# Cached attention on one core: new instruction lists, odd score steps as 64-row matmuls, query weights of 128 columns

## The chip, the core and the metric

The kernel runs on one core of a Trainium2 chip. The core has five engines with instruction streams of their own: TensorE (PE; its weight loads are listed as PEld), VectorE (DVE), ScalarE (ACT), GpSimd (POOL) and SyncE (SP), which here issues all loads and stores. TensorE reads SBUF and writes PSUM, which has 8 banks; DVE and ACT empty the banks. The engines meet only through semaphores. The metric is the device time of one execution in microseconds (us).

## The reference

```python
B, Sq, D = 8, 112, 640
H, Sk, Dh = 32, 512, 192
q = (x @ wq).reshape(B, Sq, H, Dh).transpose(0, 2, 1, 3)
scores = jnp.einsum("bhqd,bhkd->bhqk", q, k_cache) * (Dh ** -0.5)
p = softmax(scores, axis=-1)
o = jnp.einsum("bhqk,bhkd->bhqd", p, v_cache)
return o.transpose(0, 2, 1, 3).reshape(B, Sq, H * Dh) @ wo
```

All inputs are bf16: x is 8 x 112 x 640, the caches are 8 x 32 x 512 x 192 each, wq is 640 x 6144 and wo 6144 x 640. For every batch and head, queries are projected from x, compared with 512 cached keys, and the softmax weights the cached values; the heads' outputs are joined and projected.

## The kernel before, in words

The 32 heads are worked in four rounds of 8. In a round, each of the 8 batches gives two *steps* of 4 heads, so that there are 64 steps, numbered n. The steps of four batches form a *group* g (8 groups of 8 steps). What is done for a step, in the names of the program:

- Q(g, lp, c): a projection of 128 query columns for the 448 rows of four batches, 5 matmuls of 448 columns (L590), emptied by ACT into `qr` (evQ, L595). Of a head's 192 dimensions 128 fill a tile and 64 are left over; pairs of heads share a third tile. DVE copies halves of `qr` into `qh` (qc, L612 and L613), so that each 64-row half also exists on the other 64 partitions.
- scores (Sm, L635 and L637; St, L648 and L650): the 112 query rows are the weights, the transposed keys `kt` stream through, 256 columns at a time; even and odd keys go to two banks. Sm does the 128-row part of each head as 8 matmuls on the full array, St the 64 rows that are left as 8 matmuls, always two at a time on the upper and lower half of the array. Banks 0 to 3 hold the scores of a step.
- softmax: DVE copies the scores to `s_sb` and takes their extreme (smax, L663), ACT takes the exponential and its sum (exp, L668), DVE the reciprocal (rc, L680) and the product with it (norm, L672), each per head but rc.
- PT: 32 small transposes of the weights on 64-row tiles (L706), emptied by ACT and DVE into `pT_sb` (evPT, L719). For the steps 57 to 61 a transposing load from SBUF to SBUF does it instead (TD, L690).
- values: PVt for the 64 dimensions that are left over, on 64-column tiles of the array (L739), and PVm for 128 (L750), emptied by ACT into `oT_sb` (evPV, L760).
- O(g, m, part): the output projection of a group, 12 matmuls per block m in two halves (L772), added up by DVE in `accT` (oacc, L786 and L787). The last group is split up for its last batches (O6, OL); OF transposes the sum back, ACT empties it (oout) and SP stores it.

The keys of the first seven batches are loaded as they are (KN) and transposed by TensorE (KT, L561, emptied by evK, L572, on DVE or ACT); later ones come through transposing loads (K, L139). V, WQ and WO are plain loads; WO(r) fills the one buffer `wo_sb` for the groups 2r and 2r+1 and so waits for the last O of group 2r-1. x is loaded in three pieces X and transposed by TensorE (XT, L546, emptied by evX).

Nothing is scheduled at run time. The order of the work is written out in lists, one for each engine (`ORDER_PE`, `ORDER_ACT`, `ORDER_DVE`, and `ORDER_SP` for loads and stores); an engine works its list in order and waits at each entry for what the entry depends on (`Plan.run`, L35). The list of TensorE names the bank that each entry fills, and filling it waits for the evacuation of the bank's previous holder. Before the list TensorE executes 18 matmuls on zeros (L578). St and PT signal on two semaphores, one for each half of the array.

Of the kernel before, what the change touches and what calls it, by code (L numbers as in the profile page):

```python
# [11 lines left out]
class Plan:  # L12

# [6 lines left out]
    def add(self, eng, name, deps, emit, sem=None, inc=1):  # L20
        assert name not in self.ops, name
        self.ops[name] = dict(eng=eng, deps=deps, emit=emit, sem=sem or eng, inc=inc)

    def number(self):
        self.count = {}
        for eng, names in self.order.items():
            for n in names:
                o = self.ops[n]
                o["at"] = {}
                for s in o["sem"] if isinstance(o["sem"], tuple) else (o["sem"],):  # L30
                    self.count[s] = self.count.get(s, 0) + o["inc"]
                    o["at"][s] = self.count[s]
        assert sum(map(len, self.order.values())) == len(self.ops)

    def run(self, eng_name, eng, sems):  # L35
        seen = {}
        for n in self.order[eng_name]:
            o = self.ops[n]
            need = {}
            for d in o["deps"]:  # L40
# [12 lines left out]
def build_mha_kernel(nc, x, k_cache, v_cache, wq, wo, out):  # L53
# [9 lines left out]
    NP = NN // 2  # L63
# [3 lines left out]
    KS, VS, QS = 4, 3, 2 * LP  # L67
    NPL = 7
# [17 lines left out]
    with ExitStack() as es:  # L86
# [9 lines left out]
        qr = sb("qr", [128, QS, 3, SG], BF16)  # L96
        qh = sb("qh", [128, 2, 2, 4, SQ], BF16)
# [21 lines left out]
        q_flat = qr[:].rearrange("p l c s -> p (l c s)")  # L119
        late = [wq_flat[:, i * 16 * SQ:(i + 1) * 16 * SQ] for i in range(4)] + [q_flat[:, 0:16 * SQ]]  # L120
# [10 lines left out]


        def load_k(i):
            r, b = divmod(i, B)
            name = ("K", i)
# [4 lines left out]
            deps = [("St", 2 * (i - KS) + 1, 3)] if i >= KS else []  # L140
            if i == KS - 1:
                deps = [("XT", c) for c in range(4)]
            add("SP", name, deps, emit, f"mK{i % KS}", 16)

        def load_v(i):
# [5 lines left out]
            deps = [("PVm", 2 * (i - VS) + j, 1) for j in range(2)] if i >= VS else []  # L151
# [26 lines left out]
        def load_wq(r, lp, n):  # L178
# [6 lines left out]
            add("SP", ("WQ", r, lp, n), [("Q", 2 * r - 1, lp + i, c) for i in range(n) for c in range(3)] if r else [],  # L185
# [3 lines left out]
        def load_wo(r):  # L189
# [6 lines left out]

        ORDER_PE = [
# [7 lines left out]
            ("K", 2, 3, 0, "DVE", "DVE"), ("K", 1, 0, 4, "DVE", "ACT"), ("K", 1, 1, 2, "ACT", "DVE"),  # L205
# [5 lines left out]
            ("K", 3, 2, 4, "ACT", "DVE"), ("PVm", 2), ("S", 6), ("K", 4, 1, 4, "ACT", "DVE"),  # L211
            ("K", 4, 2, 6, "ACT", "DVE"), ("K", 4, 0, 4, "ACT", "DVE"), ("K", 4, 3, 0, "ACT", "DVE"),
# [3 lines left out]
            ("Q", 2, 2, 1, 4), ("K", 5, 2, 6, "ACT", "DVE"), ("S", 9), ("PVt", 5, 4), ("PVm", 5),  # L216
            ("K", 6, 2, 6, "ACT", "DVE"), ("PT", 7, 0), ("Q", 2, 2, 2, 6), ("Q", 2, 1, 1, 7), ("S", 10),
            ("PVt", 6, 6), ("PVm", 6), ("K", 6, 0, 4, "ACT", "DVE"), ("K", 6, 3, 0, "ACT", "DVE"), ("PT", 8, 6),
            ("Q", 2, 3, 1, 1), ("Q", 2, 2, 0, 0), ("PVt", 7, 5), ("PVm", 7), ("Q", 2, 3, 0, 1),
            ("K", 6, 1, 4, "ACT", "DVE"), ("PT", 9, 6), ("S", 11), ("PVt", 8, 4), ("PVt", 9, 6), ("PVm", 9),  # L220
# [317 lines left out]
        for kind, *a in ORDER_PE:  # L538
            size = {"PVt": 1, "PT": 1, "O": 3, "O6": 2, "OF": 1}.get(kind)
            if size and len(a) > size:  # L540
                bank_of[(kind, *a[:size])] = a[size]
# [498 lines left out]
```

## Time and profile before

| | |
|---|---|
| median of 3 runs | 445.71 us |
| the runs | 443.73, 445.71, 450.0 us |
| profiled execution, first to last instruction (span) | 444.4 us; nothing is recorded of it beyond the span |
| instructions | 16108, of them 6805 matmuls and as many weight loads |
| busy: TensorE, DVE, ACT | 425.1, 363.2, 344.4 us |
| loaded and stored | 122.02 MB, a mean of 275 GB/s |

Busy time of an engine is the union of its instructions. For TensorE the starts of matmuls are measured and their ends are modelled, and neighbours overlap; what a matmul costs is therefore read from the distance of two starts. A group's row gives line, engine, operation, what is written and read, the shapes and the count, then total busy time in us and the mean in ns of one, and after the second bar the idle time ahead of the group with what ended it. "Issue" marks a gap that no wait in the profile explains.

### The profile page before, as it was taken

Reading aid. Unit: us, or ns where it says so; the run is one execution under the profiler, and the core shown is the slowest. Engines: PE = TensorE matmul, PEld = TensorE weight load, DVE = VectorE, ACT = ScalarE, POOL = GpSimd, SP = SyncE. Lnnn points to the kernel's source line nnn. Section 1 sums busy time; section 2 is a strip of 40 time slices with the busy share of each in tenths; the row PEclk is TensorE's granted clock in tenths of the full one; section 3 lists DMA queues with packets and bytes.
Section 4 is the critical chain, followed back from the end, with each engine's and each line's share of the span. In section 5 each row is a group of like instructions: output and inputs, shape, how many; then the busy total and the mean of one; then the engine's idle time right before and its main releaser. Section 6 shows DMA issues by size and latency. Waiting matters only on the chain.

```text
span 444.4 us, 16108 instructions
## 1 busy us (share of the span) xinstructions
PE 425.1 (96%) x6805; PEld 304.5 (69%) x6805; DVE 363.2 (82%) x1165; ACT 344.4 (78%) x770; POOL 0.7 (0%) x6
## 2 busy tenths in 40 slices
PE   6998989889999999999899999999999999899995
PEld 4666666666677667777677766767667766676895
DVE  1579999879699889888989798889799888969871
ACT  3699999887678687978869688788778758965773
POOL 0000000000000000000000000000000000000000
PEclk9999999999999999999999999999999999989999
DMA  8999999998999999999999999999999999999952
GB/s 278 373 337 323 347 299 285 226 342 276 232 289 317 215 270 270 365 247 288 238 223 324 301 236 267 360 370 234 234 266 313 256 267 371 234 173 242 237 176 80
DMA packets 222184, 122.02 MB, mean 275 GB/s; under 512 B 164640, under 2 KB 222112, under 8 KB 222112
## 3 DMA queue, kind: packets, MB, share of 16 engines
q1 hardware_dynamic: 222112, 120.99, 106.6%
q8 instruction: 54, 0.88, 0.8%
q14 instruction: 18, 0.15, 0.1%
HBM read 78.22 MB, written 1.15 MB: 179 GB/s over the span
## 4 chain that ended last, share of the span: by engine, by line
PE 84%; DVE 5%; ACT 5%; DMA 4%; issue 2%; SPq 0%; ACTq 0%
PE ps L772 19%; PE ps L590 18%; PE ps L750 12%; PE ps L648 7%; PE ps L739 7%; PE ps L635 6%; PE ps L637 6%; PE ps L706 5%; DVE s_sb L663 3%; DMA wo_sb<-in_k_cache_dram 2%; PE ps L561 2%; ACT p_sb L668 2%; DMA wq_sb<-in_wq_dram 2%; ACT qr L595 1%; DVE p_sb L672 1%
## 5 line engine op out<-in xcount | busy, mean ns | idle before, releaser
L668 ACT ACTIVATE p_sb<-s_sb,nmx 112x512 bf16<-112x512 f32 x256 | 182.8, 717 | 31.6 <-DVE s_sb L663 26.8
L663 DVE TENSOR_SCALAR_CACHE_REDUCE s_sb<-ps 112x512 f32<-112x512 f32 x256 | 169.4, 684 | 29.6 <-PE ps L650 20.8
L590 PE MATMUL ps<-xT_sb,wq_sb 128*128 128x448 bf16 x480 | 102.0, 353 | 3.3 <-DMA wq_sb<-in_wq_dram 2.3
L772 PE MATMUL ps<-oT_sb,wo_sb 128*128 128x448 bf16 (+1 forms) x480 | 93.3, 341 | 0.1
L672 DVE TENSOR_SCALAR p_sb<-p_sb,rinv 112x512 bf16<-112x512 bf16 x256 | 81.3, 347 | 1.5
L590 PEld LDWEIGHTS ps<-xT_sb,wq_sb 128*128 128x128 bf16 x480 | 42.9, 98 | 41.5 <-DMA wq_sb<-in_wq_dram 2.9
L772 PEld LDWEIGHTS ps<-oT_sb,wo_sb 128*128 128x128 bf16 x480 | 44.3, 98 | 35.0 <-DVE pT_sb L719 0.5
L760 ACT ACTIVATE oT_sb<-ps 128x672 bf16<-128x672 f32 x64 | 46.3, 726 | 25.8 <-PE ps L750 25.4
L595 ACT ACTIVATE qr<-ps 128x448 bf16<-128x448 f32 x96 | 49.6, 539 | 12.7 <-PE ps L590 12.1
L750 PE MATMUL ps<-pT_sb,vt 128*128 128x112 bf16 x944 | 55.8, 215 | 2.0 <-issue 2.0
L719 ACT ACTIVATE pT_sb<-ps 128x768 bf16<-128x768 bf16 x59 | 47.0, 801 | 12.8 <-PE ps L706 12.8
L750 PEld LDWEIGHTS ps<-pT_sb,vt 128*128 128x128 bf16 x944 | 48.1, 99 | 6.3 <-issue 2.1
L668 ACT ACTIVATION_READ_ACCUMULATOR p_sb<-s_sb,nmx 112x1 f32 x256 | 49.5, 193 | 0.0
L719 DVE COPY pT_sb<-ps 128x1024 bf16<-128x1024 bf16 x59 | 40.3, 683 | 3.4 <-PE ps L706 2.6
L706 PE MATMUL ps<-ident,p_sb 64*128 64x64 bf16 (+1 forms) x1888 | 37.3, 185 | 1.2 <-issue 0.6
L706 PEld LDWEIGHTS ps<-ident,p_sb 64*128 64x128 bf16 (+1 forms) x1888 | 33.3, 94 | 5.8 <-DVE p_sb L672 2.0
L635 PE MATMUL ps<-kt,qr 128*112 128x256 bf16 x128 | 36.0, 282 | 0.9 <-ACT oT_sb L760 0.4
L637 PE MATMUL ps<-kt,qh 128*112 128x256 bf16 x128 | 35.2, 275 | 1.1 <-issue 1.1
L635 PE MATMUL ps<-kt,qh 128*112 128x256 bf16 x128 | 35.1, 274 | 0.0
L637 PE MATMUL ps<-kt,qr 128*112 128x256 bf16 x128 | 35.0, 274 | 0.0
L650 PE MATMUL ps<-kt,qh 64*112 64x256 bf16 x128 | 34.1, 291 | 0.1
L648 PE MATMUL ps<-kt,qr 64*112 64x256 bf16 x128 | 34.0, 291 | 0.0
(62 smaller groups left out, 478.6 us busy)
## 6 DMA issues: line engine op xcount, KB each, us to landing
vt<-in_v_cache_dram SPq DMA_DIRECT2D x32, 1536.0 KB, 9.0
wo_sb<-in_wo_dram SPq DMA_DIRECT2D x4, 1920.0 KB, 12.7
wq_sb<-in_wq_dram SPq DMA_DIRECT2D x14, 480.0 KB, 5.7
wo_sb<-in_k_cache_dram SPq DMA_DIRECT2D x3, 1536.0 KB, 9.3
accT<-in_k_cache_dram SPq DMA_DIRECT2D x3, 1536.0 KB, 12.7
vt<-in_k_cache_dram SPq DMA_DIRECT2D x2, 768.0 KB, 10.0
out_dram<-xT_sb SPq DMA_DIRECT2D x8, 140.0 KB, 3.2
wq_sb<-in_wq_dram SPq DMA_DIRECT2D x1, 960.0 KB, 10.6
```

Source lines behind the costliest of these rows:

```text
L590: mm = e.matmul(ps[:, bank, 0:SG], wq_sb[:, dc, c0:c0 + 128], xT_sb[:, dc, bh * SG:(bh + 1) * SG], start=(dc == 0), stop=(dc == DC - 1))
L595: return e.activation(qr[:, q_slot(g, lp), c, :], ps[:, bank, 0:SG], ACTF.Copy)
L635: e.matmul(ps[0:SQ, 2 * j, hs], ev, ktb[:, :, 0, cs(i)], start=(h == 0), stop=False, skip_group_check=True)
L637: mm = e.matmul(ps[0:SQ, 2 * j + 1, hs], od, ktb[:, :, 2, cs(i)], start=(h == 0), stop=False, skip_group_check=True)
L648: m1 = e.matmul(ps[0:SQ, 2 * j, hs], ev, ktb[0:64, :, 1, cs(i)], start=False, stop=True, skip_group_check=True)
L663: return e.tensor_scalar(s_sb[:, a, :].rearrange("p (e c) -> p e c", e=2), ps[0:SQ, 2 * j:2 * j + 2, h * 256:(h + 1) * 256], -scale, None, ...
L668: return e.activation(p_sb[:, k, :], s_sb[:, a, :], ACTF.Exp, bias=nmx[:, k:k + 1], scale=-1.0, accum_out=rsum[:, k:k + 1])
L672: return e.tensor_scalar(p_sb[:, k, :], p_sb[:, k, :], rinv[:, k:k + 1], None, op0=ALU.mult)
L706: ends.append(e.transpose(psb[:, bank + t, i * w:(i + 1) * w], p_sb[lo:hi, (4 * n + k) % 8, q * 128:(q + 1) * 128], ident[lo:hi, lo:hi]))
L719: return e.activation(dst, src, ACTF.Copy) if j == 0 else e.tensor_copy(dst, src)
L750: mm = e.matmul(ps[:, b0 + j, 2 * h * SQ:(2 * h + 1) * SQ], vtb[:, h0 + 2 * j + h, d0:d0 + 128], pT(j, h, q), start=(q == 0), stop=(q == 3))
L772: mm = e.matmul(ps[:, bank_of["O", g, m, 0], 0:nc_], wo_sb[:, k, m * 128:(m + 1) * 128], oT_sb[:, g % 2, k, 0:nc_], start=(k == 0), stop=( ...
```

## The change

All lists are new: the order of the entries on TensorE, ACT, DVE and SP, and the banks, which now stand in a list of their own. Some evacuations change engines (evK: 20 on ACT and 36 on DVE, before 25 and 31; evX: 2 and 5, before 4 and 3). The scores of the 25 odd steps from 15 to 63 are computed by 64-row matmuls alone: S1 covers two thirds of a head's rows, and S2, which may stand later in the list, the third with the halves of the array exchanged; 24 matmuls take the place of 16. In every step the query weights are read 128 columns wide, so 16 columns beyond the 112 of the batch; `qr` and `qh` get space for that, and four memsets on DVE clear what would be read uninitialized, ahead of the matmuls on zeros. Waits become finer: each half of a step's scores (two heads) waits for its own two banks and its own keys, and signals once. The code also gains a form of the projections in pairs of halves and a list for GpSimd; both are empty here.

```diff
+    QP = 3 * SG + 16
...
-        qr = sb("qr", [128, QS, 3, SG], BF16)
-        qh = sb("qh", [128, 2, 2, 4, SQ], BF16)
+        qr = sb("qr", [128, QS * QP], BF16)
+        qh = sb("qh", [128, 2 * 2 * 4 * SQ + 16], BF16)
...
+        ROWS = (15, 17, 19, 21, 23, 25, 27, 29, 31, 33, 35, 37, 39, 41, 43, 45, 47, 49, 51, 53, 55, 57, 59, 61, 63)
...
+        def q_at(n, j, c, lo, hi):
+            c0 = (q_slot(group(n), 2 * qd) + j) * QP + c * SG + b % (B // 2) * SQ
+            return qr[lo:hi, c0:c0 + 128]
+
+        def h_at(n, j, k, lo, hi):
+            c0 = ((n % 2 * 2 + j) * 4 + k) * SQ
+            return qh[lo:hi, c0:c0 + 128]
...
+            def mm(e, j, h, odd, q, blk, lo, hi, first, last):
+                hs = slice(h * 256, (h + 1) * 256)
+                return e.matmul(ps[:, 2 * j + odd, hs], q, ktb[lo:hi, :, blk, cs(2 * j + h)],
+                                start=first, stop=last, skip_group_check=True)
...
+                def straight(e, j=j):
+                    for h in range(2):
...
+                        for i in range(2):
+                            a = mm(e, j, h, 0, ev[i], i, 0, 64, f and i == 0, False)
+                            b = mm(e, j, h, 1, od[i], 1 + i, 64, 128, f and i == 0, False)
+                    return a, b
+
+                def swapped(e, j=j):
+                    for h in range(2):
+                        od, ev = ((h_at(n, j, 1, 0, 64), q_at(n, j, 0, 64, 128)) if h == 0 else
+                                  (q_at(n, j, 2, 0, 64), h_at(n, j, 2, 64, 128)))
+                        a = mm(e, j, h, 1, od, 2, 0, 64, False, True)
+                        b = mm(e, j, h, 0, ev, 0, 64, 128, False, True)
+                    return a, b
...
+                if n in ROWS:
+                    add("PE", ("S1", n, j), [("qc", n)] + keys, straight, ("PE", "PE2"))
+                    add("PE", ("S2", n, j), [("S1", n, j)], swapped, ("PE", "PE2"))
+                else:
+                    add("PE", ("Sm", n, j), [("qc", n)] + keys, mains)
+                    add("PE", ("St", n, j), [], rests, ("PE", "PE2"))
...
-                add("DVE", ("smax", n, i), [("St", n, 2 * j + 1), ("exp", *old)], smax)
+                add("DVE", ("smax", n, i), [("S2" if n in ROWS else "St", n, j), ("exp", *old)], smax)
...
-                add("DVE", ("rc", n, j), [("exp", n, 2 * j), ("exp", n, 2 * j + 1)], rc)
+                add("DVE", ("rc", n, j), [("exp", n, 2 * j), ("exp", n, 2 * j + 1),
+                                          ("norm", n - 2, 2 * j), ("norm", n - 2, 2 * j + 1)], rc)
...
+            e.memset(qr[:].rearrange("p (l w) -> p l w", w=QP)[:, :, 3 * SG:QP], 0.0)
+            e.memset(qh[0:64, 0:16 * SQ].rearrange("p (j k s) -> p j k s", j=4, k=4)[:, :, 0, :], 0.0)
+            e.memset(qh[64:128, 0:16 * SQ].rearrange("p (j k s) -> p j k s", j=4, k=4)[:, :, 3, :], 0.0)
+            e.memset(qh[:, 16 * SQ:], 0.0).then_inc(zINIT, 1)
...
-            ("X", 0), ("X", 1), ("WQ", 0, 1, 1), ("WQ", 0, 0, 1), ("KN", 0, 0, 4), ("X", 2), ("WQ", 0, 2, 2),
+            ('X', 0), ('WQ', 0, 0, 1), ('X', 1), ('KN', 0, 0, 4), ('WQ', 0, 1, 1), ('WQ', 0, 2, 2), ('X', 2),
...
-            ("V", 23), ("V", 25), ("K", 28), ("K", 27), ("K", 29), ("V", 27), ("V", 26), ("WO", 3), ("V", 28),
-            ("K", 30), ("K", 31), ("TD", 57), ("TD", 58), ("V", 29), ("TD", 59), ("V", 30), ("TD", 60), ("TD", 61),
+            ('V', 25), ('V', 26), ('K', 28), ('K', 29), ('K', 30), ('V', 27), ('V', 28), ('V', 29), ('K', 31), ('TD', 57),
+            ('TD', 58), ('WO', 3), ('TD', 59), ('V', 30), ('TD', 60), ('TD', 61), ('V', 31), ('OUT', 0), ('OUT', 4),
...
+            ('St', 58, 0), ('St', 58, 1), ('PT', 56), ('O', 5, 0, 1), ('O', 5, 2, 1), ('S1', 59, 0), ('S1', 59, 1),
+            ('S2', 59, 0), ('S2', 59, 1), ('O', 5, 4, 0), ('O', 5, 4, 1), ('PVt', 55), ('PVm', 55, 0), ('PVm', 55, 1),
+            ('Sm', 60, 0), ('Sm', 60, 1), ('St', 60, 0), ('St', 60, 1), ('PVt', 57), ('PVt', 58), ('PVm', 57, 0),
+            ('PVm', 57, 1), ('PVm', 58, 0), ('PVm', 58, 1), ('S1', 61, 0), ('S1', 61, 1), ('PVt', 56), ('S2', 61, 0),
+            ('S2', 61, 1), ('PVm', 56, 0), ('PVm', 56, 1), ('O', 6, 1, 0), ('O', 6, 4, 0), ('O', 6, 4, 1), ('O', 6, 1, 1),
```

More of the change, by code (lines that the diff above doesn't have):

```diff
@@ L535, in build_mha_kernel, with x_transposes @@
             add("SP", ("OUT", b), [("oout", b)], emit, f"mOUT{b % DC}", 16)
[L537 to L543 removed]
+        bank_of = {tuple(t): b for t, b in BANKS}
+        def x_transposes(c):
+            bank = bank_of["XT", c]
             def emit(e):
@@ L602, in q_of, with q_pair, emit @@
-        def q_of(n):
+                    w, v = q_tile(g, lp, c, dc, 0, 128)
+                    mm = e.matmul(ps[:, bank, 0:SG], w, v, start=(dc == 0), stop=(dc == DC - 1))
+                return mm
+            add("PE", ("Q", g, lp, c), q_need(g, lp), emit)
+            q_evac(g, lp, c)
+        def q_pair(i):
+            pair = QPAIRS[i]
+            banks = [bank_of["Q", *u] for u in pair]
+            def emit(e, swap):
+                for dc in range(DC):
+                    ends = []
+                    for t in range(2):
+                        w, v = q_tile(*pair[t ^ swap], dc, 64 * t, 64 * t + 64)
+                        ends.append(e.matmul(ps[:, banks[t ^ swap], 0:SG], w, v, start=(dc == 0 and not swap),
+                                             stop=(dc == DC - 1 and bool(swap)), skip_group_check=True))
+                return tuple(ends)
+            need = [d for u in pair for d in q_need(*u[:2])]
+            add("PE", ("Qs", i), need, lambda e: emit(e, 0), ("PE", "PE2"))
+            add("PE", ("Qw", i), [("Qs", i)], lambda e: emit(e, 1), ("PE", "PE2"))
+            for u in pair:
+                q_evac(*u)
@@ L844, in emit @@
                 return mm
-            add("DVE", ("oaccL", part), [("OL", 1, part)], emit)
+            add("DVE", ("oaccL", part), [("OL", 1, part)] + [("oacc", NG - 3, m) for m in range(DC)], emit)
         def o_final(b):
@@ L959, in build_mha_kernel @@
+        order["PE"], order["ACT"], order["DVE"] = ORDER_PE, ORDER_ACT, ORDER_DVE
+        order["POOL"], order["SP"] = ORDER_POOL, ORDER_SP
+        holder = {}
+        for op in ORDER_PE:
+            for bank, evacs in tiles(op):
+                P.ops[op]["banks"] = P.ops[op]["banks"] + holder.get(bank, [])
+                holder[bank] = evacs
         P.number()
```

769 lines of the change are left out of this document (367 added, 402 removed), and 199 rows, old and new, of tables (BANKS, ORDER_PE, ORDER_SP).

## The prediction

> **What bounds the kernel now.** I read the page first, then the groups of TensorE by shape, then a table of stretches, then the instructions in order of time inside one step.
>
> ```profile
> span 444.4 us, 16108 instructions
> PE 425.1 (96%) x6805; PEld 304.5 (69%) x6805; DVE 363.2 (82%) x1165; ACT 344.4 (78%) x770; POOL 0.7 (0%) x6
> PE 84%; DVE 5%; ACT 5%; DMA 4%; issue 2%; SPq 0%; ACTq 0%
> 17.50:124.70 107.20, 100.36 (x1875) 70.12 (x1875) 90.26 (x282) 92.29 (x201) 0.00 (x0) 1.00 1.05 296
> 124.70:372.70 248.00, 246.12 (x3776) 174.20 (x3775) 216.15 (x700) 196.41 (x449) 0.00 (x0) 1.00 1.16 283
> 372.70:444.40 71.70, 64.47 (x1017) 51.31 (x1014) 52.43 (x174) 48.68 (x109) 0.00 (x0) 0.97 0.86 203
> 40.00:80.00 40.00, 36.04 (x817) 26.93 (x816) 37.76 (x120) 38.12 (x84) 0.00 (x0) 1.00 1.08 315
> ```
>
> The third line is the chain that ended last: 84% TensorE. The stretches (length, then busy time of PE, weight loads, DVE, ACT, POOL, then clock, DMA share, GB/s) are the time from the scores of step 0 to those of step 15, from there to step 55, and the rest. In the middle TensorE is idle for 1.9 of 248 us: there, only what TensorE executes counts. In the first stretch it idles 6.8 us, and between 40 and 80 us DVE (37.76 of 40) and ACT (38.12) are full: the start is held by the two softmax engines, which also empty the transposed K. In the last stretch 7.2 us are idle.
>
> What a step's scores cost is read from start times, since the ends are modelled:
>
> ```profile
> 125.37 0.27 PE L635 MATMUL ps<-kt,qh 128*112 128x256 bf16 x1
> 125.48 0.27 PE L637 MATMUL ps<-kt,qr 128*112 128x256 bf16 x1
> 125.68 0.31 PE L648 MATMUL ps<-kt,qr 64*112 64x256 bf16 x1
> 125.68 0.31 PE L650 MATMUL ps<-kt,qh 64*112 64x256 bf16 x1
> 125.83 0.27 PE L648 MATMUL ps<-kt,qh 64*112 64x256 bf16 x1
> 125.94 0.27 PE L648 MATMUL ps<-kt,qr 64*112 64x256 bf16 x1
> 126.05 0.27 PE L648 MATMUL ps<-kt,qh 64*112 64x256 bf16 x1
> 126.16 0.63 PE L706 MATMUL ps<-ident,p_sb 64*128 64x64 bf16 x32
> PEld ps L648 <- issue: 11.4, 64, 0.2
> ```
>
> A full-height matmul (L635, L637) takes 0.11 us; a pair of 64-row ones (L648 with L650, started together) also 0.11. From the last full one to the first pair it is 0.20, so changing the array's shape costs 0.09. The first pair after the change takes 0.15: its successor's weights could not be loaded beforehand. The wait row (total, times, longest) shows that this happens in all 64 steps.
>
> **The change, part by part.** The sum is made against the profiled execution, whose time is known only as its span, 444.4; the median of the runs is 445.7, 1.3 above it, and I carry differences over unchanged.
>
> *Shape changes.* Full array, 64-row tiles and 64-column tiles alternate; counting neighbours of unlike shape along the old and the new list of TensorE gives 254 and 238 changes. 16 x 0.09 = **-1.5**. An odd step now changes shape on entry, not between its two halves, and the transposes L706, 64-row too, often stand inside it. At 0.04 to 0.13 each the bounds are -0.6 and -2.1.
>
> *64-row scores.* An old step issues 8 full matmuls and 4 pairs, 12 slots of 0.11; a new odd step issues 12 pairs, again 12 slots. 200 more matmuls, no more time: **0**. Nothing shows a pair below 0.11; if each paid the 0.15 of the first pair, it would be 25 x 12 x 0.04 = +12, the upper bound. I take the row of the steady pairs, which is three of the four.
>
> *128 columns.*
>
> ```profile
> L637 PEld LDWEIGHTS ps<-kt,qr 128*112 128x112 bf16 x128 | 16.8, 131 | 0.0
> L650 PEld LDWEIGHTS ps<-kt,qr 64*112 64x112 bf16 x128 | 16.2, 126 | 0.0
> L590 PEld LDWEIGHTS ps<-xT_sb,wq_sb 128*128 128x128 bf16 x480 | 42.9, 98 | 41.5 <-DMA wq_sb<-in_wq_dram 2.9 <-ACT kt L572 1.0 <-issue 0.6
> L706 PEld LDWEIGHTS ps<-ident,p_sb 64*128 64x128 bf16 x944 | 33.2, 95 | 5.0 <-DVE p_sb L672 2.0 <-ACT oT_sb L760 0.9 <-issue 0.5
> ```
>
> A load of 128 columns takes 95 or 98 ns, one of 112 takes 126 or 131: the wider one is 31 ns shorter. Behind a 0.11 us matmul this is hidden; it is worth something only where the load stands bare, once a step: 64 x 0.03 = **-2.0**, between 0 and 64 x 0.04 = -2.6. The Trainium skill, "TensorE: Matmul & The Clock Gate", section on LDWEIGHTS, gives a load's time as its columns divided by 1.2 in ns, which speaks against this edit: 107 against 93 ns, +0.9 us as an estimate of that page instead of -2.0. Its section on Fast Weight Load says that exactly 128 columns of a type that is not FP32 switch on a quicker load; the four rows agree with that and not with the first rule.
>
> *Waits in the middle.*
>
> ```profile
> L760 ACT ACTIVATE oT_sb<-ps 128x672 bf16<-128x672 f32 x64 | 46.3, 726 | 25.8 <-PE ps L750 25.4
> ```
>
> The new lists reorder everything between steps 15 and 55, where TensorE is idle for 1.9 us; they can win that or lose as much again: -1.9 to +1.9. A bank of PSUM can be refilled when it has been emptied, 0.73 us for the values' product plus the signals on both sides. Summing slots along the lists, the new one comes back to a bank after 0.95 us of other TensorE work at the earliest, the old one in four places after 0.69 to 0.79; four times the 0.2 to 0.3 that is missing there is **-1.0**. The waits that the change adds in code (each half of the scores for its own two banks, the reciprocal for the normalization two steps back on its own engine) have nothing late behind them that was not awaited before.
>
> *The start.*
>
> ```profile
> 7.66 1.12 PE L590 MATMUL ps<-xT_sb,wq_sb 128*128 128x448 bf16 x5 [1.97 <-DMA wq_sb<-in_wq_dram]
> L572 DVE COPY kt<-ps 128x768 bf16<-128x768 bf16 x31 | 16.5, 551 | 10.5 <-PE ps L561 10.5
> L572 ACT ACTIVATE kt<-ps 128x768 bf16<-128x768 bf16 x25 | 19.7, 817 | 4.9 <-PE ps L561 4.7
> L786 DVE COPY accT<-ps 128x448 f32<-128x448 f32 x10 | 6.2, 618 | 0.3 <-PE ps L772 0.3
> 343.02 2.27 PE ps L772 x12
> 349.58 0.94 PE ps L590 x5
> ```
>
> Ahead of step 15's scores the old list has 38 projections Q and 10 halves of O, the new 36 and 1. By the last two rows (chain of waits; 12 matmuls are two halves) 9 x 1.13 + 2 x 0.94 = 12.1 us of TensorE work move behind step 15. They are not saved. DVE keeps its work: five K evacuations more (5 x 0.55), five accumulations fewer (5 x 0.62), so 90.0 us of the 90.3; ACT loses five of 0.82 and is no longer the fuller one. If DVE is 94% full, as between 40 and 80 us, step 15 comes 90.0/0.94 = 95.7 us after step 0 instead of 107.2: 11.5 earlier, 12.1 to be paid later, +0.6. At 90% it is +4.9, with no gap -5.1. At the very start the second block of x now follows the first weights in the load queue. The first projection (7.66, released by its weights) needs all three either way, but then transposes and evacuations come after the last of them; later projections no longer wait for a second weight load: +0.2. Four new memsets delay the warm-up matmuls, under the same loads. Together **+0.8**, from -5 to +6.
>
> *The end.* The last output weights, WO 3, overwrite those that the O of group 5 read, and stood in the load queue ahead of V 28 and of the transposing loads TD. Now they stand behind TD 57 and TD 58, and the old weights' last use (O, 5, 4, 1) is late:
>
> ```profile
> wo_sb<-in_wo_dram SPq DMA_DIRECT2D x4, 1920.0 KB, 12.7
> DMA to landing us min/median/max: 10.2/12.7/14.7
> wq_sb<-p_sb SPq DMA_TRANSPOSE x4, 4.6
> 368.30 0.98 PE L739 MATMUL ps<-pT_sb,vt 128*64 128x112 bf16 x32
> 369.21 1.75 PE L750 MATMUL ps<-pT_sb,vt 128*128 128x112 bf16 x32
> 370.99 0.64 PE L706 MATMUL ps<-ident,p_sb 64*128 64x64 bf16 x32
> ```
>
> Between (O, 5, 4, 1) and (O, 6, 1, 0), the first reader, the new list has two steps of scores (1.45 each, 124.71 to 126.16 in the step above) and the values of four steps (2.69 for two, 368.30 to 370.99): 8.3 us. The second row is the four landings of such a load. So TensorE waits 1.9, 4.4 or 6.4 us by the shortest, median or longest; every later instruction of TensorE is queued behind. K and V are mostly landed by then, so I take the shortest: **+1.9**, from 0 (the softmax engines may stretch the 8.3) to +8. PVt 58 also waits for TD 58, 4.6 us after a step's normalization; that wait lengthens the 8.3 by as much as it costs, so it isn't added.
>
> Sum: -1.5 + 0 - 2.0 - 1.0 + 0.8 + 1.9 = **-1.8**: 442.6 against the span, 443.9 against the median.
>
> **The rivals.**
>
> *The start is freed.* ACT was the fuller engine there by 2 us and loses 5; if DVE then runs without gaps the start gives -5.1, the middle its -1.9, and WO lands in time: -1.5 - 2.0 - 1.9 - 5.1 = -10.5, 435.2. For it: only DVE and ACT are full there. Against it: both fill each other's buffers, and 94% is the best this trace shows.
>
> *WO 3 is late; slower than before.* Without the last term the sum is -3.7, so this decides from a wait of 3.7 us on, which the median landing already gives. With the longest landing it is 6.4, and a long gap costs clock:
>
> ```profile
> 387.28 1.96 issue
> 390.00:400.00 10.00, 10.00 (x126) 7.57 (x121) 6.28 (x21) 6.26 (x15) 0.00 (x0) 0.85 0.89 160
> 391.69 0.42 PE L635 MATMUL ps<-kt,qr 128*112 128x256 bf16 x1
> 391.90 0.42 PE L637 MATMUL ps<-kt,qh 128*112 128x256 bf16 x1
> ```
>
> After a gap of 2 us the granted clock was 0.85 over the next 10 us and full matmuls came 0.21 apart instead of 0.11: 10 x 0.15 = 1.5 us lost. 6.4 + 1.5 - 3.7 = +4.2: 449.9. Against it: the load ring is emptier there than at any of the four loads measured. By the skill's "TensorE: Matmul & The Clock Gate", section on the clock gate, it takes an idle window of about 3.4 us; the trace shows the drop after 2.
>
> *64-row pairs cost 0.15 each,* since a step of nothing but pairs loads two sets of weights per slot: +12, hence 455.9. Against it: three pairs of four run at 0.11 with the slower 112-column loads.
>
> *The wider weights show nothing* (the load was not what the 0.15 consists of): 445.9; within the forecast's range.
>
> **How the numbers follow.** Forecast 0.5 (438 to 447), start freed 0.2 (431 to 438), WO late 0.2 (447 to 453), slow pairs 0.08, anything else 0.02. The range 434 to 452.5 leaves out the slow pairs and about a third of the freed start. 2% of 445.7 is 8.9 us, about what a measurement of this kernel can tell from no change: faster than 436.8 is 0.15, slower than 454.6 is 0.10, the rest 0.75.
>
> **What would show it.** In the profile after: weight loads of the scores at 95 to 98 ns; pairs of an odd step 0.11 apart; 0.12 instead of 0.15 after a change of shape; step 15 near 113 us; a gap of TensorE ahead of the first O of group 6, released by the load of wo. I am wrong if pairs stretch, if step 15 comes after 118 or before 109, or if TensorE idles over 4 us between steps 15 and 55.

## The result and the profile after

The changed kernel takes 461.4 us (median of 4 runs, 456.1 to 461.7) against 445.3 for the kernel before beside it: a ratio of 1.032, 95% interval 1.023 to 1.040. It is slower, and outside the range I gave. Some executions of one kernel take 1.5% and more longer than its fastest, at a lower granted clock (of the kernel before, 450 to 455 us); the medians count them, the ratios leave them out. The profiled execution has a span of 459.8 us, 15.4 more than before.

First the lines of its page that answer to those of before: span, busy time, and the chain that ended last.

```profile
span 459.8 us, 16572 instructions
PE 429.0 (93%) x7005; PEld 290.1 (63%) x7005; DVE 366.3 (80%) x1176; ACT 342.4 (74%) x763; POOL 0.7 (0%) x6
PE 73%; DVE 13%; DMA 6%; issue 4%; ACT 2%; SPq 0%; DVEq 0%; ACTq 0%
```

TensorE has as much to do as before (429.0 against 425.1), but its share of the chain fell from 84 to 73%; DVE, transfers and gaps that nothing explains ("issue") have taken it. Next the same three stretches as in the prediction: step 0's scores to step 15's, to step 55's, to the end (length, busy PE, weight loads, DVE, ACT, POOL, clock, DMA share, GB/s).

```profile
20.30:121.20 100.90, 88.49 (x1811) 61.52 (x1809) 88.40 (x279) 85.73 (x187) 0.00 (x0) 0.98 0.94 283
121.20:378.10 256.90, 253.15 (x3996) 166.74 (x3996) 220.41 (x713) 202.95 (x464) 0.00 (x0) 1.00 1.15 276
378.10:459.80 81.70, 70.54 (x1073) 51.69 (x1065) 52.66 (x170) 46.41 (x101) 0.00 (x0) 0.98 0.78 196
```

Step 0 begins 2.8 us later, step 15 comes 101.0 us after it (before 107.2), and TensorE idles 12.4 us of the first stretch instead of 6.8. Since work moved from one stretch to the next, I set each against its own work: the entries of TensorE's list in that stretch, each at the distance of starts that it has where nothing waits (a projection 0.946 us, a half of O 1.135, a step's scores 1.45 before and 1.42 after, and so on). What is left over is waiting.

| stretch | before: length, work, waits | after: length, work, waits | waits more |
|---|---|---|---|
| to step 0 | 17.5 | 20.3 | 2.8 |
| step 0 to 15 | 107.2, 96.9, 10.3 | 101.0, 83.6, 17.4 | 7.1 |
| step 15 to 55 | 248.0, 244.0, 4.0 | 256.8, 247.6, 9.2 | 5.2 |
| step 55 to the last matmul | 66.8, 61.4, 5.4 | 78.1, 67.1, 11.0 | 5.6 |

The work itself fell by 4.0 us (402.3 to 398.3 in the three stretches). The waits grew by 20.7, and what follows the last matmul's start is 1.3 shorter (3.6 after, 4.9 before): 20.7 - 4.0 - 1.3 is the 15.4 of the span. No single place lost the time.

**In the start** the gaps of TensorE are mostly "issue", gaps that no wait explains. The rows are the waits of TensorE's matmuls in that stretch, first after, then before (total, times, longest):

```profile
PE ps L892 <- issue: 2.2, 1, 2.2
PE ps L691 <- issue: 1.8, 1, 1.8
PE ps L643 <- issue: 1.6, 2, 1.1
PE ps L643 <- ACT kt L133: 1.6, 1, 1.6
PE ps L848 <- issue: 1.5, 1, 1.5
```

```profile
PE ps L561 <- issue: 2.0, 2, 1.1
PE ps L706 <- issue: 0.6, 1, 0.6
```

I counted the records of TensorE's two queues (matmuls, weight loads, their semaphore entries) ahead of these gaps. After: 705, 1217, 2499, 2753, 3010 and 3266. Before: 1473, 2754, 3266, and later 7106 and 12226. Divided by 256 every one of them leaves 193, 194 or 195: they stand whole multiples of 256 instructions apart. The gap at 705 is the fourth row, put down to an evacuation of K, but the entry there, KT(2, 2), waits only for evacuations that had ended by 29.1 us; its first weight load ran at 29.12, and its first matmul came at 30.85. Up to step 15 the gaps sum to 8.7 us after (1.55, 2.16, 0.55, 1.49, 1.10, 1.83) and 2.6 before (0.56, 0.87, 1.13), 6.1 of the 7.1. Behind the one of 2.16 us the granted clock was 0.50 from 47.0 to 50.4 us (before it was 1.00 there), which costs up to half of these 3.4 us.

The trace also shows what ends these gaps. The page lists a DMA queue of instructions (packets, MB, share):

```profile
q8 instruction: 55, 0.90, 0.8%
```

These are 55 packets of 16 KB, about one for every 256 of TensorE's 14213 records. Each of the six gaps ends 1.3 to 1.5 us after such a packet has ended, and these six packets began 3.2 to 7.0 us after TensorE had passed the preceding place of this kind.

**In the middle** the waits are many and short. The stretch is longer in every profile of the table with the new lists: 256.1 to 262.0 us without e10_free_order, against 246.7 to 250.4 in the three with the lists of before. Some of the weight loads' waits from step 15 to 55 follow, after and then before, without the rows of "issue". The transposes (L848, L706) wait for the normalization, the values (L880, L739) for P's evacuation, the scores (L747, L635) for the row maxima, and S2 for its own S1 (fourth row).

```profile
PEld ps L848 <- DVE p_sb L813: 3.2, 8, 0.6
PEld ps L880 <- ACT pT_sb L133: 2.2, 6, 0.4
PEld ps L747 <- DVE s_sb L804: 2.4, 8, 0.4
PEld ps L747 <- PE ps L747: 1.3, 6, 0.2
```

```profile
PEld ps L706 <- DVE p_sb L672: 1.2, 5, 0.4
PEld ps L739 <- ACT pT_sb L719: 0.8, 2, 0.5
PEld ps L635 <- DVE s_sb L663: 0.6, 3, 0.3
```

**At the end** one chain is seen. First SP's queue after (start, length, operation), then the chain of waits.

```profile
380.35 5.42 SPq L153 DMA_DIRECT2D vt<-in_v_cache_dram  x3
385.82 15.25 SPq L142 DMA_TRANSPOSE kt<-in_k_cache_dram  x1
401.11 4.18 SPq L832 DMA_TRANSPOSE wq_sb<-p_sb  x2
405.34 1.10 SPq L196 DMA_DIRECT2D wo_sb<-in_wo_dram  x1
```

```profile
400.13 0.87 DVE p_sb L813 x3
401.11 6.03 DMA wq_sb<-p_sb
407.22 0.82 ACT p_sb L809 x2
408.07 0.71 DVE s_sb L804 x2
408.83 2.00 PE ps L747 x12
421.58 6.69 DMA wq_sb<-p_sb
428.36 0.82 ACT p_sb L809 x2
429.96 1.19 PE ps L747 x16
```

V 27 to V 29 are issued, then the transposing load K 31 holds the queue for 15.25 us, then TD 57 follows and lands 6 us later. (The normalizations in the first row are step 58's; the last one of step 57 ended at 398.3, so the queue held TD 57 back by 2.8 us.) The tile p_sb has room for two steps, so exp 59 overwrites what TD 57 reads and waits for it; the last row maximum of step 59 waits for the room that exp 59 frees, and the second half of step 60's scores for this maximum, whose bank it fills. TensorE stands still for 4.6 us there and then works at half clock (granted 0.51 from 408.8 to 412.3): 12 matmuls of scores take 2.00 us (fifth row), 0.21 apart in the part that was full height. The last three rows are the same chain once more: exp 62 waits for TD 60, and TensorE for 2.4 us inside step 63. Before, TD 57 was issued at 398.3, 2.8 us earlier, step 60 was due 1.6 us later, and WO 3 had gone out at 366:

```profile
366.01 0.37 SPq L193 DMA_DIRECT2D wo_sb<-in_wo_dram  x1
370.99 0.37 SPq L150 DMA_DIRECT2D vt<-in_v_cache_dram  x1
371.40 22.36 SPq L139 DMA_TRANSPOSE kt<-in_k_cache_dram  x2
398.29 4.36 SPq L690 DMA_TRANSPOSE wq_sb<-p_sb  x2
```

### The profile page after: what moved, and what is told of

It reads as the page before. It is cut to its first block, busy times and chain, and to the rows that moved or that the text cites. A ratio compares the mean times of both kernels' runs of the same rounds, so it can differ in the third digit from the quotient of the medians.

```text
span 459.8 us, 16572 instructions
## 1 busy us (share of the span) xinstructions
PE 429.0 (93%) x7005; PEld 290.1 (63%) x7005; DVE 366.3 (80%) x1176; ACT 342.4 (74%) x763; POOL 0.7 (0%) x6
## 4 chain that ended last, share of the span: by engine, by line
PE 73%; DVE 13%; DMA 6%; issue 4%; ACT 2%; SPq 0%; DVEq 0%; ACTq 0%
PE ps L691 18%; PE ps L747 16%; PE ps L914 14%; PE ps L892 10%; DVE s_sb L804 6%; PE ps L880 6%; PE ps L848 5%; DMA wq_sb<-p_sb 3%; DVE p_sb L813 2%; PE ps L643 2%; DMA wq_sb<-in_wq_dram 2%; DMA kt<-in_x_dram 1%; ACT p_sb L809 1%; DVE pT_sb L134 1%; DVE qh L733 1%
## 5 line engine op out<-in xcount | busy, mean ns | idle before, releaser
L747 PE MATMUL ps<-kt,qr 64*128 64x256 bf16 (+1 forms) x612 | 102.0, 273 | 7.9 <-DVE s_sb L804 7.5
L691 PE MATMUL ps<-xT_sb,wq_sb 128*128 128x448 bf16 x480 | 104.7, 360 | 3.8 <-issue 1.8
L747 PE MATMUL ps<-kt,qh 64*128 64x256 bf16 (+1 forms) x612 | 95.3, 272 | 0.0
L747 PEld LDWEIGHTS ps<-kt,qr 64*128 64x128 bf16 (+1 forms) x612 | 50.8, 95 | 29.7 <-DVE s_sb L804 12.4
L133 ACT ACTIVATE qr<-ps 128x448 bf16<-128x448 f32 x96 | 50.2, 537 | 19.7 <-PE ps L691 19.1
L747 PEld LDWEIGHTS ps<-kt,qh 64*128 64x128 bf16 (+1 forms) x612 | 50.5, 95 | 7.1 <-PE ps L747 2.2
L848 PE MATMUL ps<-ident,p_sb 64*128 64x64 bf16 (+1 forms) x1888 | 37.6, 185 | 4.1 <-issue 3.1
L848 PEld LDWEIGHTS ps<-ident,p_sb 64*128 64x128 bf16 (+1 forms) x1888 | 33.1, 94 | 12.5 <-DVE p_sb L813 5.0
L880 PE MATMUL ps<-pT_sb,vt 128*64 128x112 bf16 x944 | 33.2, 215 | 2.1 <-ACT qr L133 0.8
L880 PEld LDWEIGHTS ps<-pT_sb,vt 128*64 128x64 bf16 x944 | 25.6, 109 | 15.1 <-issue 4.6
## 6 DMA issues: line engine op xcount, KB each, us to landing
vt<-in_v_cache_dram SPq DMA_DIRECT2D x32, 1536.0 KB, 10.3
vt<-in_k_cache_dram SPq DMA_DIRECT2D x2, 768.0 KB, 10.3
```

The source lines that it names most:

```text
L133: return e.activation(dst, src, ACTF.Copy)
L691: mm = e.matmul(ps[:, bank, 0:SG], w, v, start=(dc == 0), stop=(dc == DC - 1))
L747: return e.matmul(ps[:, 2 * j + odd, hs], q, ktb[lo:hi, :, blk, cs(2 * j + h)], start=first, stop=last, skip_group_check=True)
L848: ends.append(e.transpose(psb[:, bank + t, i * w:(i + 1) * w], p_sb[lo:hi, (4 * n + k) % 8, q * 128:(q + 1) * 128], ident[lo:hi, lo:hi]))
L880: mm = e.matmul(ps[64 * h:64 * h + 64, b0 + j, SQ:2 * SQ], vtb[:, h0 + 2 * j + h, d0:d0 + 64], pT(j, h, q), start=(q == 0), stop=(q == 3))
```

## The experiments

All stretches come from the profile of one execution each (start of step 0, then lengths in us; the last ends with the last matmul); the ratio is to the kernel before, with its interval.

| run | step 0 | 0 to 15 | 15 to 55 | 55 to end | median | ratio |
|---|---|---|---|---|---|---|
| before | 17.5 | 107.2 | 248.0 | 66.8 | 445.3 | 1 |
| after | 20.3 | 101.0 | 256.8 | 78.1 | 461.4 | 1.032 (1.023 to 1.040) |
| e3_again | 17.6 | 108.1 | 246.7 | 66.8 | 444.6 | 0.998 (0.994 to 1.002) |
| e4_old_rows | 17.7 | 110.5 | 250.4 | 64.2 | 448.1 | 0.999 (0.994 to 1.004) |
| e5_new_norows | 18.0 | 102.6 | 258.4 | 73.7 | 461.9 | 1.033 (1.025 to 1.042) |
| e2_start | 18.3 | 99.4 | 257.5 | 80.2 | 460.0 | 1.030 (1.025 to 1.036) |
| e9_no_loads | 17.5 | 97.8 | 256.1 | 80.3 | 457.6 | 1.026 (1.016 to 1.036) |
| e1_tail | 17.7 | 101.6 | 257.1 | 80.4 | 462.9 | 1.036 (1.031 to 1.042) |
| e11_no_td | 20.6 | 100.7 | 256.6 | 69.7 | 453.9 | 1.012 (0.998 to 1.026) |
| e7_tail_v | 19.1 | 101.0 | 259.5 | 78.6 | 463.9 | 1.039 (1.032 to 1.046) |
| e10_free_order | 18.3 | 101.4 | 279.3 | 75.4 | 480.6 | 1.075 (1.066 to 1.084) |
| e12_tail_groups | 19.1 | 99.5 | 257.8 | 78.1 | 461.6 | 1.035 (1.024 to 1.046) |
| e14_v29_last | 20.7 | 100.0 | 262.0 | 78.9 | 463.9 | 1.037 (1.026 to 1.048) |
| e15_v29_start | 18.5 | 99.2 | 258.0 | 78.5 | 460.0 | 1.033 (1.026 to 1.040) |
| e16_no_wo3 | 18.7 | 101.8 | 259.1 | 72.4 | 457.5 | 1.024 (1.015 to 1.034) |

### The lists, or the forms?

The lists and banks of before in the code of after:

```diff
-        ROWS = (15, 17, 19, 21, 23, 25, 27, 29, 31, 33, 35, 37, 39, 41, 43, 45, 47, 49, 51, 53, 55, 57, 59, 61, 63)
+        ROWS = ()
-        ORDER_PE = [ ... ]    (ORDER_ACT, ORDER_DVE, ORDER_SP, BANKS too)
+        ORDER_PE = [ ... ]    (the lists of before)
```

> All lists and banks of the kernel before, scores in 128-row and 64-row parts in every step as before; of the change there are left the query weights of 128 columns (with the zeros they read), the score parts signalled in two instead of four, and the finer waits. Theory (the lists are what lost the time): 64 steps by 0.03 us, 443.2 us, within 441 to 445.5. Rival (the wider weights or the waits cost something): 447 us or more. Rival (the wider weights show nothing): 445 us.

Measured 445.4 us, ratio 0.9965 (0.9927 to 1.0003), -1.6 us. Because the interval ended at no change, it was run again:

> The kernel with the lists of before and the query weights of 128 columns again, in five rounds, since its first interval (0.9927 to 1.0003) just reaches no change. Theory (0.033 us less in each of 64 steps): ratio 0.995, within 0.992 to 0.998. Rival: no difference, 1.000 within 0.003.

0.998 (0.9937 to 1.0024). The two together make about -1.2 us. That is the sign of the theory and most of its size, but neither interval excludes zero. In the trace each step's scores take 1.415 us instead of 1.448: the 0.033 forecast. The lists are what lost the time; which of them, or the banks, no run separates. This is also the fastest version that I ran, and no better than before by what can be told.

The same with the odd steps from 15 on as 64-row tiles (ROWS as in the change, S1 and S2 where the step's scores stood):

> As the run with the lists of before, and the odd steps from 15 on as 64-row tiles in the same place of TensorE's list. Theory (the 64-row form itself is nearly free): the same 24 slots of two instructions, one change of shape less in each of these 25 steps (0.09 us) and a wait of 0.06 to 0.15 us on the first half of the same step, so within 1.5 us of the run with the lists of before. Rival (the 64-row form lost the time): at least 5 us above that run, or 0.2 us and more in each of 25 steps.

448.1 us, ratio 0.999, so 0.0026 or 1.2 us above the run without, with intervals that overlap: the form is nearly free. In each of the 25 steps the first half of S2 takes 0.34 us and the second 0.22, 3.2 us in all, where the second half waits until its S1 has ended. No shape changes are saved here: this list has 254, as the one without the form. And the reverse, the new lists without the form (S1 becomes Sm, S2 becomes St):

> All lists of the changed kernel, but every step's scores in 128-row and 64-row parts again. Theory (the lists lost the time, the 64-row form costs about 1 us, as the two runs with the lists of before differ): 460 to 463 us. Rival (in these lists the second half of a step's 64-row pairs waits for its own first half and for the row maxima, 0.1 to 0.3 us in each of 25 steps, and that is a third of the loss): 454 to 458 us.

461.9 us: the form is not what made the new lists slow either. The profile is of the fastest of its four executions (458.0, the others 461.2 to 462.8); whether its shorter last stretch, 73.7 us, comes from the form or from chance is not shown.

### The start

```diff
-            ('X', 0), ('WQ', 0, 0, 1), ('X', 1), ('KN', 0, 0, 4), ('WQ', 0, 1, 1), ('WQ', 0, 2, 2), ('X', 2),
+            ('X', 0), ('X', 1), ('WQ', 0, 0, 1), ('KN', 0, 0, 4), ('WQ', 0, 1, 1), ('WQ', 0, 2, 2), ('X', 2),
-            ('evX', 0), ('evQ', 0, 0, 0), ...    (ACT)
+            ('evX', 0), ('evX', 3), ('evQ', 0, 0, 0), ...
```

> The second slice of x is loaded second again, ahead of the first query weights, and its first evacuation goes to ScalarE, so that the two no longer follow each other on VectorE. Theory (the start's delay is carried to the end): step 0's scores begin at 17.5 to 18.2 us in place of 20.3, and the time falls by 2 to 2.8 us, to 458.6 to 459.6 us. Rival (the later loads of K and V and the queue at the end set the pace): step 0 comes earlier but the time stays within 1 us of the changed kernel's 461.4.

460.0 us, 1.4 below the changed kernel, between theory and rival, and the intervals overlap. Step 0 began at 18.3. But the nine runs with the changed start have it anywhere from 17.5 to 20.7 (mean 19.0), those with the start of before between 17.4 and 17.7, and the three with this edit at 18.3 to 18.7. So the new start costs 0 to 3 us at random, and this edit is worth about half a microsecond of it; the 2.8 us of the profiled execution were partly chance.

What makes the gaps at every 256th instruction? Ten loads are left out:

```diff
-            ('V', 3), ('V', 4), ('K', 7), ('K', 8), ('V', 5), ('V', 6), ('V', 7), ('K', 10), ('V', 8), ('K', 9)
```

> V 3 to V 8 and K 7 to K 10 are left out, steps 6 to 21 compute with what the tiles hold. From about 55 to 110 us only KN, WQ and WO are still loaded; nothing in TensorE's list changes. Five gaps of TensorE that nothing in the trace explains stand in the changed kernel at 30.9, 46.7, 85.9, 94.0 and 100.5 us, 1.1 to 2.2 us each, at instructions 705, 1217, 2753, 3010 and 3266 of its list, whole multiples of 256 apart. Theory (the next 256 instructions are fetched over the same DMA engines and come late when these are loaded): the gaps at 2753, 3010 and 3266 fall from 1.1 to 1.8 us to under 0.4 us each, those at 705 and 1217 stay, and step 15 begins some 4 us earlier after step 0, near 97 us. Rival (the gaps belong to those places in the list whatever is loaded): all five stay at 1 us and more. The time as a whole falls for other reasons too, since later loads come earlier.

The gaps at 2753, 3010 and 3266, which summed to 4.4 us, are gone (none over 0.2), and so is the smaller one at 2499. In the nine other executions with the same list and loads up to there these four come to 2.7 to 5.3 us. The gaps at 705 (2.26) and 1217 (1.89), where all loads still run, stay. Step 15 comes 97.8 us after step 0, 3.2 earlier than in the changed kernel; the nine others have 99.2 to 102.6. The matmuls' waits for "issue" in the start are now this one row:

```profile
PE ps L892 <- issue: 1.9, 1, 1.9
```

So the gaps depend on what is loaded, and the theory holds. The packets of the instruction queue show it too: those for 2499 to 3266 begin 0.4 to 1.5 us after the preceding place is passed, where in the changed kernel it is 3.9 to 5.6. They take about 1 us each in both runs, so it is their start that is late. The Trainium skill, "Runtime: NRT & Kernel Launch", section "Instruction fetch mechanics", says that an engine's instructions are refilled in blocks of 256 by a DMA queue of their own, mostly hidden. The 256 agrees with these gaps; hidden it is not while loads run: 0.6 to 2.2 us each in the changed kernel.

### The end

K 31 alone, ahead of V 28 instead of behind V 29:

```diff
-            ..., ('V', 27), ('V', 28), ('V', 29), ('K', 31), ('TD', 57),
+            ..., ('V', 27), ('K', 31), ('V', 28), ('V', 29), ('TD', 57),
```

> Only K 31's transposing load is moved, from behind V 29 to ahead of V 28 in SP's list. Theory (the queue at the end): in the changed kernel this load held SP for 15.25 us (385.82 to 401.07), TD 57 was issued at 401.1 though its last norm ended near 395.6, and the waits that follow from it on exp 59, on the row maxima and on TensorE come to about 9 us after 403 us. With the load issued near 381, TD 57 goes out at 396 to 398 and the time falls by 5 to 9 us, to 452 to 456 us. Rival (VectorE and ScalarE set the pace of the last steps whatever the queue does): the gap before step 60's second half moves but the end does not, 459 to 461 us. A second rival: the load only changes places, and V 28, V 29 and TD 57 queue behind it in the same way, 460 to 462 us.

462.9 us. The chain of waits shows the second rival, though the time is 0.9 above its range: TD 57 went out 3.8 us earlier and landed no sooner.

```profile
397.35 10.68 DMA wq_sb<-p_sb
408.11 0.82 ACT p_sb L809 x2
408.96 0.71 DVE s_sb L804 x2
409.71 2.00 PE ps L747 x12
```

How much hangs on the TD at all? They are left out:

```diff
-            if n in BY_DMA:
-                p_by_dma(n)
-            else:
-                transposes(n)
+            if n not in BY_DMA:
+                transposes(n)
```

> The five transposing transfers of P (TD 57 to 61) are left out: the values of steps 57 to 61 are multiplied with what the query weights' tile holds, so that part of the output is not computed. Nothing then waits for these transfers. Theory (the end lost its time to them): the waits of 4.6 and 2.4 us of TensorE at steps 60 and 63, and the half clock behind the first (matmuls 0.21 apart for 3.4 us, about 1.7 us), go: 451 to 454 us. Rival (VectorE and ScalarE are late there by themselves): 457 us or more.

453.9 us, 7.5 less; the stretch from step 55 on shrinks from 78.1 to 69.7. The theory holds for this part, and both waits, 4.6 and 2.4 us, are gone. Since nothing waits for the TD here at all, that is the most that their lateness can cost. By the ratio, 1.012, some 5 us above the kernel before are left, in an interval from none to 12.

Two orders by the time at which a load's place comes free, for the last eight loads and for all from K 7 on:

```diff
-            ('V', 26), ('K', 28), ('K', 29), ('K', 30), ('V', 27), ('V', 28), ('V', 29), ('K', 31), ('TD', 57),
+            ('K', 28), ('V', 26), ('K', 29), ('V', 27), ('K', 30), ('V', 28), ('K', 31), ('V', 29), ('TD', 57),
```

> The last eight loads ahead of TD 57 stand in the order in which their places come free (K 28, V 26, K 29, V 27, K 30, V 28, K 31, V 29). Moving K 31 alone gave nothing: TD 57 was issued 4 us earlier but its data came behind those of V 28 and V 29 and landed at 408. Theory (these loads are late because V 27 and V 28, free near 357 and 369 us, stand behind K 30, which waits until 371 us): with them 10 us earlier the transfers are done when TD 57 is issued, it lands 4 to 5 us after its issue near 396, and the time falls by 4 to 6 us, to 455 to 458. Rival (TensorE's list has only 3.8 us of work between step 59 and the second half of step 60, so it waits there whatever the loads do): less than 2 us.

> From K 7 on every load of SP's list stands in the order in which its place comes free by TensorE's list. Theory (loads that are held behind others whose place is not free lose the time in the whole second half): as the run with the last eight loads reordered, and 1 to 3 us more from fewer waits in steps 8 to 55: 452 to 456 us. Rival (no wait in steps 15 to 55 comes from a load): no better than that run, within 1 us of it.

463.9 and 480.6 us: theory and rivals both missed. In the second, a K between two plain loads holds SP's queue for 7 to 13.5 us, mostly over 10, where the kernel with V 29 moved and WO 3 left out (below) shows one behind two other K in 6.6:

```profile
304.05 13.09 SPq L142 DMA_TRANSPOSE kt<-in_k_cache_dram  x1
317.18 0.58 SPq L153 DMA_DIRECT2D vt<-in_v_cache_dram  x1
317.86 12.47 SPq L142 DMA_TRANSPOSE kt<-in_k_cache_dram  x1
330.38 0.58 SPq L196 DMA_DIRECT2D wo_sb<-in_wo_dram  x1
```

```profile
338.85 6.59 SPq L142 DMA_TRANSPOSE kt<-in_k_cache_dram  x1
```

A pair of K and V then takes 13.8 us (304.05 to 317.86), two steps of the middle 12.8 in the changed kernel (256.8/20) and 14.0 in this run (279.3/20): with one kind after the other the loads become the bound. TensorE waited 11.4 us for WQ and 5.5 for WO in that run.

```profile
PE ps L692 <- DMA wq_sb<-in_wq_dram: 11.4, 3, 9.5
PE ps L915 <- DMA wo_sb<-in_wo_dram: 5.5, 1, 5.5
```

So the next order kept loads of one kind together (K 28, K 29, V 26, V 27, V 28, K 30, K 31, V 29):

> The last eight loads ahead of TD 57 stand in groups of one kind, K 28, K 29, V 26, V 27, V 28, K 30, K 31, V 29, so that no transposing load of K is issued between two loads of V (in the order by free places each such K held SP for 11 to 16 us). Theory (the end lost its time to transfers that were behind when TD 57 was issued): K 31 is issued by 390 us, TD 57 lands by 402, and the time falls by 4 to 7 us, to 454 to 457 us; leaving all TD out gave 453.9. Rival (the transfers take as long in any order and TD 57 comes behind them again): 459 us or more.

461.6 us, as the rival has it; its chain has TD 57 from 397.74 on for 9.56 us, until 407.3. In four orders of these loads it was issued at 397 to 401 and landed at 407 to 411, which fits that the bytes ahead of it set when it comes. Therefore fewer bytes, as in the kernel before:

```diff
-            ('V', 29), ('K', 31), ('TD', 57), ('TD', 58), ('WO', 3), ('TD', 59), ...
+            ('K', 31), ('TD', 57), ('TD', 58), ('V', 29), ('WO', 3), ('TD', 59), ...
-            ..., ('PVt', 57), ('PVt', 58), ..., ('S1', 61, 1), ('PVt', 56), ...
+            ..., ('PVt', 57), ('PVt', 56), ..., ('S1', 61, 1), ('PVt', 58), ...
```

> V 29 is loaded behind TD 57 and TD 58, as in the kernel before, and because step 58 needs it, its values change places with those of step 56 in TensorE's and ScalarE's lists. Four orders of the loads ahead of TD 57 left it landing at 407 to 410 us; here 1.5 MB less are ahead of it. Theory (what counts is the bytes that stand ahead of TD 57 after K 31's place comes free): TD 57 lands by 403, TensorE waits less than 1 us in step 60 in place of 4.6, and the time falls by 4 to 6 us, to 455 to 458 us (all TD left out gave 453.9). Rival (K 31 alone keeps the transfers busy until 401 and TD 57 lands at 406 or later, or V 29 is now what the values wait for): 460 us or more.

463.9 us, with other gaps in its middle; its four executions came at 460.3, 460.8, 467.1 and 468.0. The same with the start's edit:

> The same with the second slice of x loaded second and its first evacuation on ScalarE. Theory (the start's 2 us and the end's 5 add up): 453 to 456 us. Rival (the first loads vary by themselves, step 0 began between 17.5 and 20.6 us in the runs with the changed start): as the run without this edit, within 1 us.

460.0 us, within 1 us of the lower two executions without the edit, which is what the rival says. In both the wait in step 60 is gone and the stretch from 55 on is as long as ever (78.9 and 78.5), for now O of group 6 waits for WO 3. In the last run (waits of TensorE, then the matmuls behind the gap in order of time):

```profile
PE ps L927 <- DMA wo_sb<-in_wo_dram: 4.4, 1, 4.4
```

```profile
415.18 7.21 PE L927 MATMUL ps<-oT_sb,wo_sb 128*128 128x448 bf16 x24 [4.35 <-DMA wo_sb<-in_wo_dram]
```

```profile
416.85 4.70 PE L914 MATMUL ps<-oT_sb,wo_sb 128*128 128x448 bf16 x24
```

The last row is the changed kernel's, without a gap before it: the lower clock (granted 0.50 from 413.5 to 420.3) costs 2.5 us more. The last run leaves WO 3 out too:

```diff
-            ('K', 31), ('TD', 57), ('TD', 58), ('V', 29), ('WO', 3), ('TD', 59), ...
+            ('K', 31), ('TD', 57), ('TD', 58), ('V', 29), ('TD', 59), ...
```

> As the run with V 29 behind TD 58 and x second, and the load of WO 3 is left out: groups 6 and 7 of the output projection multiply with the weights of the round before. With V 29 moved, TD 57 came in time and TensorE waited 4.4 us for WO 3 instead, with matmuls at half clock behind it (6.26 us for 24 that take 4.70 elsewhere). Theory (the end is bound by the bytes that must be loaded between step 55, when K 31's place comes free, and step 62, whichever of them comes last): the wait of 4.4 us and the slow matmuls go and nothing takes their place, 453 to 455 us. Rival (the next late transfer, TD 59 or V 30, takes the place of WO 3): 458 us or more.

457.5 us, between the ranges of theory and rival. The stretch from 55 on falls by 6.1 to 72.4, as the theory has it, but not without a successor: V 29 is now in the chain, and TensorE waits 2.5 us for it:

```profile
404.02 9.15 DMA vt<-in_v_cache_dram
```

The time fell by only 2.5, with intervals that overlap, since the other stretches came out 3.9 longer in this execution.

What follows: from step 55 on, when K 31's place comes free, the end is bound by K 31, V 28, V 29, TD 57, TD 58 and WO 3 together. The order only decides which of them TensorE waits for. Before, step 55 came 5.4 us earlier, step 60 1.6 later, and WO 3 was loaded already, since the halves of O that read its predecessor were done ahead of step 54; the new list has them until step 59. That moving them forward would shorten the end was not tried.

## Why the prediction was wrong

In the terms of the sum the profile gives -4.0 for the work (the first three), +5.2 for the middle, +9.9 for the start (2.8 and 7.1), +5.6 for the end up to the last matmul and -1.3 behind it: +15.4 in place of -1.8.

*Shape changes, -1.5.* Not measured by themselves; the price after a change is as forecast. The first two pairs of an odd step behind a half of O:

```profile
144.91 0.28 PE L747 MATMUL ps<-kt,qr 64*128 64x256 bf16 x1
144.91 0.28 PE L747 MATMUL ps<-kt,qh 64*128 64x256 bf16 x1
145.02 0.27 PE L747 MATMUL ps<-kt,qr 64*128 64x256 bf16 x1
```

0.12 to the next pair in place of 0.15. Together with the next two terms the work fell by 4.0 us, and 3.5 was forecast.

*64-row scores, 0, and 128 columns, -2.0.* Right in the traces: pairs are 0.11 apart, and score weights load in 94 to 98 ns. The runs gave +1.2 for the form and about -1.2 for the columns together with the finer waits, neither clear of zero. The forecast left out that S2 waits for S1.

```profile
L747 PEld LDWEIGHTS ps<-kt,qh 64*128 64x128 bf16 x456 | 35.2, 94 | 3.8 <-PE ps L747 2.2
L747 PEld LDWEIGHTS ps<-kt,qh 128*128 128x128 bf16 x156 | 15.3, 98 | 3.3
```

*Waits in the middle, -1.0 with bounds of 1.9 either way.* Wrong: +5.2. The step that failed is to look at one kind of wait only, the banks that come free, and to take the idle time of before as the bound on both sides. What grew are, among others, the waits from normalization to transpose, from evacuation to values and from maxima to scores. No run tried these; where the 5.2 us come from is shown by rows, not by an experiment.

*The start, +0.8 with a reach to +6.* The mechanism was right (12 us of work move behind step 15), the size was not. Step 15 came 101.0 us after step 0, not 95.7, with DVE busy 88.4 of 100.9 us: 88%, where I took 94. I had 90% as +4.9 and gave it no case of its own. The step that failed is the 94%, taken over from 40 us of the old trace. What kept DVE from being full was not among my terms, TensorE's waits for its own instructions above all: 8.7 us, 6.1 more than before, and the half clock behind one of them. The first row shown under the rival of a late WO 3, 387.28 1.96 issue, was such a gap (12226), and I did not ask what it was. The first loads, put at +0.2, cost 2.8 here and 0 to 3 elsewhere.

*The end, +1.9.* Wrong, by "K and V are mostly landed by then". K 31 was being issued until 401. I looked for the one load whose place comes free late, WO 3, and followed what waits for it. I did not see that exp 59 waits for TD 57, nor add up what must be loaded from step 55 on. The rival's price for WO 3 is still what one finds when TD 57 is out of the way: 4.4 us and 2.5 of clock, where the rival had 6.4 and 1.5.

The rival on the slower side was thus the right mechanism at the wrong load, and it came with the two other terms at or beyond their upper bounds. The range summed terms as if only one could go wrong. All lists came from one rearrangement, so their waits went the same way together.

## To carry to other kernels

When work is moved in a schedule, add up for each stretch what the loads need between the time their places come free and the time their data is needed. Here a queue that was busy nearly all the time had no free order, and taking one wait away only showed the next. Where every list is new at once, sum the waits of the old trace by kind and allow each kind to change, and several in the same direction; the idle time of before was no bound here. Where a gap has no wait that explains it, count the instructions ahead of it: here every such gap stood at a multiple of 256 from the next. Of a dependency through a small ring of buffers (here two steps of P), name the reader that frees it, and when that reader's own input can be issued.

## What the runs showed of the hardware

- TensorE's gaps that no wait explains stand whole multiples of 256 instructions apart, 0.6 to 2.2 us each and 8.7 us up to step 15 in the changed kernel. Each ends 1.3 to 1.5 us after a packet of 16 KB in the instruction queue. With ten loads left out four of them, 5.0 us, were gone.
- A transposing load of K (1.5 MB) held SP's queue for 5.9 to 8.1 us behind another of its kind and for 8.7 to 15.8 behind a plain load (all of the changed kernel). The Trainium skill, "DMA: Bandwidth & Descriptors", section "Latency and other measured facts", gives 261 GB/s for transposing loads; 1.57 MB in 6.6 us are 238, near it. The order by free places, which alternates both kinds, took 480.6 us against 461.4.
- A gap of 4.4 us was followed by 7.21 us for 24 matmuls that take 4.70 otherwise, and gaps of 2.0 (before) and 2.2 us (after, at 46.7) by 3.4 us at a granted clock of 0.5.
- The start of the same lists varied by 3 us from execution to execution (17.5 to 20.7), that of the lists before by 0.3.
